# Reading the last 64 rows of the second wq as eight groups of sixteen half rows

## The chip, the cores and the metric

The kernel runs on one core of a Trainium2 chip. The metric is the device time of one execution in microseconds, here the median of three runs. One further execution was taken by the hardware profiler; durations and times of single steps come from it.

## What is computed

Two independent problems, A and B, of the same shapes are computed one after the other: one decoding step of attention over a sliding window. Per problem:

```python
# x [2, 1, 576], k_cache and v_cache [2, 16, 16384, 128], wq [576, 4096], wo [4096, 576], all bf16
W = 4096                                     # the last 4096 positions of the cache
q = (x @ wq).reshape(B, 1, 32, 128)          # 32 query heads, 16 key heads
scores = einsum(q, k[last W]) * 128 ** -0.5  # each key head serves two query heads
o = einsum(softmax(scores), v[last W])
result = o.reshape(B, 1, 4096) @ wo          # [2, 1, 576]
```

The output is both results side by side.

## The kernel before

Nearly all of the data is read once: per problem 32 MB of keys, 32 MB of values and twice 4.5 MB of weights. The caches are read as slabs of 4 MB, `K0` to `K15` and `V0` to `V15` (eight of each per problem); a slab holds one key head in each of four (batch, head group) places, with 32 KB for each of 128 partitions. Slabs go into the ring buffer `ring`, which has four places. Everything large is issued by SyncE (SP) on one queue, in the order of a list `stream`: both wq first, then K0, K1, V0, K2, V1 and so on, and at the end K14, K15, V13, V14, V15. A slab's issue (line 246) waits for the last reader of the slab four places before. The last slab, V15, comes in two pieces (line 242), of 96 and 32 of its 128 columns of keys, each with a semaphore of its own; behind it stand the last rows of wo (lines 282 and 267). The small outputs of problem A are issued on the same queue after that (line 708).

Per K slab, VectorE transposes the slab in four parts (`xt`, line 460), TensorE computes scores (`st`, lines 483 and 167), VectorE takes the maximum, ScalarE the exponential, and VectorE lays the result out for the product with the V slab (`acc`, line 575). That product runs one to two slabs behind. ScalarE evicts it (`acc_sb`, line 587), TensorE combines it (`ot`, line 604, for the last slab line 594), and after every second slab a projection with wo follows (line 690). The outputs are cast (lines 698 and 699) and written (line 708).

The queries come first. wq has 576 rows. Its first 512 are read as one slab of 4 MB into `ring` (line 255), four rows to a partition. The last 64 rows have 8 KB each; they are read in half rows of 4 KB, one to each of 128 partitions, into `wqr` (line 253): partition 2r + h holds half h of row r. A column of the first half of the output may use only the partitions of the first half rows. So the matching column of x is spread with zeros: `x_dup` holds two vectors of 128 values, one for each half h, with x at the partitions 2r + h and 0 at the others. `f_xd` (line 361) writes x into them, TensorE transposes them together with the four chunks of the rest of x (line 354), ScalarE copies the six results into `xT` (line 369), and line 413 multiplies chunk by chunk.

Of the kernel before, what the change touches and what calls it, by code (L numbers as in the profile page):

```python
# [6 lines left out]
BF16 = mybir.dt.bfloat16  # L7
# [52 lines left out]
def build_kernel(nc, probs, out, cfg=None):  # L60
# [8 lines left out]
    NPROB = len(probs)  # L69
    Bb, _one, D = x0.shape  # L70
# [15 lines left out]
    NFC = D // 128  # L86
    DREM = D - 128 * NFC
    assert DREM * 2 == 128 and NFC * HD == SLABW
    HH = HD // 2
    NXC = NFC + 2  # L90
    NOUT = wo0.shape[1]
    NH = NOUT // 2
    ACC0 = 128
# [12 lines left out]
    with es:  # L106
        block = es.enter_context(nc.Block())
        sb = lambda name, shape, dt: es.enter_context(nc.sbuf_tensor(name, shape, dt))
        ring = sb("ring", [128, NR, SLABW], BF16)
        xt = sb("xt", [128, NKT, 2048], FP32)  # L110
        wqr = sb("wqr", [128, NPROB, HH], BF16)
        wob = sb("wob", [128, 2, 8, NOUT], BF16)
        xT = sb("xT", [128, NXC, NPROB, 128], BF16)
        x_dup = sb("x_dup", [NPROB * Bb, 2, DREM, 2], BF16)
        x_sb = sb("x_sb", [NPROB * Bb, D], BF16)
        ident_b = sb("ident_b", [128, 128], BF16)
        zq = sb("zq", [128, 4, NZQ, ZW], BF16)
# [40 lines left out]
        wq_sem = [sem("wq%d" % r) for r in range(NPROB)]  # L158
# [6 lines left out]
        def matmul_again(e, first, out_ap, rhs, start, stop, skip=True):  # L165
            i = first.ins
            return e.add_instruction(mybir.InstMatmult(  # L167
                name=nc.get_next_instruction_name(), engine=i.engine, ins=[e.lower_ap(rhs), i.ins[1]], outs=[e.lower_ap(out_ap)],
                start_tensor_calc=start, stop_tensor_calc=stop, tile_size=i.tile_size, tile_position=i.tile_position,
                bass_skip_group_check=skip, ldweights=False))  # L170

        S = _Sched()
        dma_count = {}

        def dma_op(eng, sem_h, n_dmas, fn, deps, tag):
            op = S.add(eng, fn, deps, tag)
            dma_count[sem_h] = dma_count.get(sem_h, 0) + 16 * n_dmas
            op.dma = (sem_h, dma_count[sem_h])
            return op

        def load_x(P, eng):
            return dma_op(eng, x_sem[P], 1, lambda e: e.dma_start(
                x_sb[P * Bb:(P + 1) * Bb, :], probs[P][0][:, 0, :]).then_inc(x_sem[P], 16), [], "xload%d" % P)
# [14 lines left out]
        p_mrow = S.add("pool", lambda e: e.affine_select(  # L198
            mrow[:].rearrange("k (x c r) -> k x c r", c=4, r=2), ones_b[0:4, :].rearrange("k (x c r) -> k x c r", c=4, r=2),
            [[0, 16], [1, 4], [0, 2]], ALU.is_equal, 0.0, base=0, channel_multiplier=-1), [p_ones_b], "mrow")  # L200
        x_zd = S.add("dve", lambda e: e.memset(x_dup[:].rearrange("b h r t -> b (h r t)"), 0.0), [], "zero_xdup")

        stream = [("Q", P) for P in range(NPROB)]
        for s_ in range(ND + LS):
# [44 lines left out]
        def issue_wq(n, P):  # L249
            wqP = probs[P][3]  # L250
            r = n % NR
            deps = [reader[n - NR]] if n >= NR else []
            wq_dma[P] = dma_op("sp", wq_sem[P], 1, lambda e: e.dma_start(
                wqr[:, P, :], wqP[NFC * 128:D, :].rearrange("r (h n) -> r h n", h=2)).then_inc(wq_sem[P], 16), [], "wqr%d" % P)
            slab_dma[n] = dma_op("sp", ring_sem[r], 1, lambda e: e.dma_start(
                ring[:, r, :], wqP[0:NFC * 128, :].rearrange("(p s) n -> p (s n)", s=NFC)).then_inc(ring_sem[r], 16), deps, "wq%d" % P)

            if P == 0:
                for P_ in range(1, NPROB):
                    x_dma[P_] = load_x(P_, "sp")  # L260
# [27 lines left out]
        def issue_until(n_needed):  # L288
            while nxt[0] <= n_needed:
                for G in w_at.pop(stream[nxt[0]], []):  # L290
                    issue_wo(G)
                issue_slab(nxt[0])
                nxt[0] += 1
# [25 lines left out]
        def tb_job(fn, tag, deps):  # L319
            n = tbn[0]  # L320
            tbn[0] += 1
            bank = TB[n % NTB]
            d = list(deps)
            if n >= NTB:
                d.append(tb_consumer[n - NTB])
            return n, bank, S.add("pe", lambda e: fn(e, bank), d, tag)
# [18 lines left out]
        def f_xT(e, bank):  # L345
            last = None
            bb = bank[:].bitcast(BF16)
            NB = NPROB * Bb
            for ch in range(NXC):
                if ch < NFC:  # L350
                    src = x_sb[0:NB, 0:NFC * 128].rearrange("b (p s) -> b s p", s=NFC)[:, ch, :]
                else:
                    src = x_dup[0:NB, ch - NFC, :, :].rearrange("b r t -> b (r t)")
                last = e.transpose(bb[:, ch * NB:(ch + 1) * NB], src, ident_b[0:NB, 0:NB])  # L354
            return last
        issue_until(0)
        init_small()
        def f_xd(e):
            last = None
            for hf in range(2):  # L360
                last = e.tensor_copy(x_dup[:, hf, :, hf], x_sb[:, NFC * 128:D])  # L361
            return last
        x_cd = S.add("dve", f_xd, [x_zd] + list(x_dma.values()), "xdup")

        n_x, bank_x, op_xT = tb_job(f_xT, "xT", list(x_dma.values()) + [x_cd, p_ident_b])

        def f_xev(e):
            NB = NPROB * NXC
            return e.activation(
                xT[:].rearrange("c h p (a w) -> c (h p) a w", a=4)[:, :, :, 0:Bb],  # L370
                bank_x[:].bitcast(BF16)[:, 0:NB * Bb].rearrange("c (p b) -> c p b", b=Bb).unsqueeze(2).broadcast_to([128, NB, 4, Bb]),
                ACTF.Copy)
# [22 lines left out]
        def do_qproj(G):  # L395
            P = G // GPP
            nq = pos[("Q", P)]
            issue_until(nq)
            evs = []
            for nb in range(2):  # L400
                hf = nb
                c0 = nb * HH + 512 * (G % GPP)

                def fn(e, bank, c0=c0, hf=hf, nb=nb):
                    last = None
                    chs = list(range(NFC - 1)) + [NFC, NFC - 1]
                    for k_, ch in enumerate(chs if nb == 0 else chs[::-1]):
                        w_ = ring[:, nq % NR, ch * HD + c0:ch * HD + c0 + 512] if ch < NFC else wqr[:, P, c0 - hf * HH:c0 - hf * HH + 512]
                        x_ = xT[:, ch if ch < NFC else NFC + hf, P, :]
                        if k_ == 0 and q_first[0] == (P, ch):  # L410
                            last = matmul_again(e, q_first[1], bank[:, 0:512], w_, True, False, False)
                        else:
                            last = q_first[1] = e.matmul(bank[:, 0:512], x_, w_, start=(k_ == 0), stop=(k_ == NFC))  # L413
                        q_first[0] = (P, ch)
                    return last
                n, bank, op = tb_job(fn, "q%d_%d" % (G, nb), [slab_dma[nq], wq_dma[P], op_xev])
                qproj[(G, nb)] = op
                reader[nq] = op
                d = [op]
                if G >= 1:  # L420
                    d.append(chain[(G - 1, "qtr")])
                evs.append(S.add("act", lambda e, bank=bank, nb=nb: e.activation(qrow[:, 512 * nb:512 * nb + 512], bank[:, 0:512], ACTF.Copy),  # L422
                                 d, "qrow%d_%d" % (G, nb)))
                tb_consumer[n] = evs[-1]
            d = list(evs)
            if G >= 1:
                d.append(qkeep[G - 1])
            chain[(G, "qtr")] = S.add("dve", lambda e: e.transpose(qtr[:].bitcast(FP32), qrow[:].bitcast(FP32)), d, "qtr%d" % G)  # L428

            def f_keep(e):  # L430
                last = None
                v = qtr[:].rearrange("d (t l r f w p) -> d l w t r f p", t=2, l=2, r=2, f=2, w=32)
                o = qk[:, G, :, :, :].rearrange("d l (f p) (b t r) -> d l b t r f p", f=2, b=Bb, t=2)
                for l_ in range(2):
                    for b in range(Bb):
                        last = e.activation(o[:, l_, b], v[:, l_, b], ACTF.Copy)  # L436
                return last
            qkeep[G] = S.add("act", f_keep, [chain[(G, "qtr")]], "qkeep%d" % G)
# [358 lines left out]
        for e in ENGS:  # L797
            n = 0
# [77 lines left out]
def bass_concat_heads__sliding_block_cached__sliding_block_cached__decode_kernel(  # L876
    nc, A_x, A_k_cache, A_v_cache, A_wq, A_wo, B_x, B_k_cache, B_v_cache, B_wq, B_wo, out,
):
    build_kernel(nc, [(A_x, A_k_cache, A_v_cache, A_wq, A_wo), (B_x, B_k_cache, B_v_cache, B_wq, B_wo)], out)
# [28 lines left out]
```

## Time and profile before

| | |
|---|---|
| median of three runs | 366.08 us (365.82 to 366.17) |
| profiled execution, first to last instruction (span) | 364.5 us |
| median less span | 1.6 us |
| DMA | 153.27 MB, 420 GB/s over the span |
| PE busy | 219.7 us (60%) |
| DVE busy | 198.6 us (54%) |
| ACT busy | 67.8 us (19%) |
| POOL busy | 16.4 us (4%) |
| chain that ended last | DMA 70%, DVE 14%, PE 12%, ACT 2% |

PE is TensorE's matrix multiplication, PEld its loading of weights, DVE VectorE, ACT ScalarE, POOL GpSimd and SP SyncE. A row of the timeline has its start, its duration, the engine, the line, the operation, what it writes and reads, the shape, how many there are in one row, and in brackets how long the engine had been idle before and what ended that. The chain that ended last is followed back from the last instruction, at each step to what released it. The profile has no time of its own for the profiled execution beyond its span; the runs' median is set beside it.

### The profile page before, as it was taken

The numbers are of one execution on the slowest core, as the hardware profiler recorded it, in microseconds if no ns is written. First come the engines' busy times: TensorE is split into PE (matmuls) and PEld (weight loads), VectorE is DVE, ScalarE is ACT, GpSimd is POOL, SyncE is SP. The second block draws the span as 40 slices with busy tenths as digits, with TensorE's granted clock in tenths as the row PEclk, the third lists the DMA queues.
The fourth block names the chain that finished last, engine by engine and source line by source line (L and its number), as shares of the span: only waits on it lengthen the run. The fifth ranks groups of instructions, "written<-read, shape, count | busy, mean of one in ns | idle before, by whom it ended". The sixth has DMA issues, their size and how long they took to land.

```text
span 364.5 us, 2971 instructions
## 1 busy us (share of the span) xinstructions
PE 219.7 (60%) x1370; PEld 64.7 (18%) x1097; DVE 198.6 (54%) x173; ACT 67.8 (19%) x155; POOL 16.4 (4%) x45
## 2 busy tenths in 40 slices
PE   0399687291837657192955749083764828286866
PEld 0023112020211212021211212021221202021132
DVE  2022895574909375382917568291926557199620
ACT  1047203020300303020200303020210303011211
POOL 5000000000000000000000000000000000000000
PEclk9999899697885969687685969889696969869985
DMA  8999999999999999999999999999999999999993
GB/s 345 432 432 435 428 409 457 414 453 408 440 435 428 433 412 447 424 433 428 427 445 421 442 424 424 430 432 432 422 450 421 442 421 423 439 421 442 415 419 136
DMA packets 7075, 153.27 MB, mean 420 GB/s; under 512 B 780, under 2 KB 1304, under 8 KB 1688
## 3 DMA queue, kind: packets, MB, share of 16 engines
q1 hardware_dynamic: 7056, 153.10, 98.1%
q8 instruction: 9, 0.15, 0.2%
q10 hardware_dynamic: 8, 0.00, 0.0%
q14 instruction: 2, 0.02, 0.0%
HBM read 153.10 MB, written 0.00 MB: 420 GB/s over the span
## 4 chain that ended last, share of the span: by engine, by line
DMA 70%; DVE 14%; PE 12%; ACT 2%; issue 0%; SPq 0%; DVEq 0%
DMA ring<-in_B_k_cache_dram 34%; DMA ring<-in_A_k_cache_dram 25%; DVE xt L460 13%; DMA ring<-in_B_v_cache_dram 8%; PE st L483 4%; PE st L167 3%; DMA x_sb<-in_B_x_dram 3%; PE tb L413 3%; ACT qrow L422 1%; PE tb L167 1%; DVE qtr L428 1%; PE ot L690 1%; DVE nM L506 1%; ACT qk L436 0%; PE tb L496 0%
## 5 line engine op out<-in xcount | busy, mean ns | idle before, releaser
L460 DVE STREAM_TRANSPOSE xt<-ring 128x2048 f32<-128x2048 f32 x64 | 144.9, 2285 | 108.3 <-DMA ring<-in_B_k_cache_dram 59.4
L483 PE MATMUL st<-xt,zq 128*128 128x512 bf16 x256 | 113.0, 442 | 121.5 <-DVE xt L460 121.2
L167 PE MATMUL st<-xt,zq 128*128 128x512 bf16 x256 | 111.9, 437 | 0.0
L483 PEld LDWEIGHTS st<-xt,zq 128*128 128x128 bf16 x256 | 27.3, 107 | 209.7 <-DVE xt L460 138.5
L511 ACT ACTIVATE nMrep<-nM 1x128 f32<-1x128 f32 x16 | 4.9, 308 | 176.5 <-DVE nM L506 176.5
L575 PE MATMUL acc<-ring,pC 128*32 128x512 bf16 x512 | 34.1, 403 | 1.3 <-DMA ring<-in_B_v_cache_dram 1.3
L536 DVE STREAM_TRANSPOSE pC<-pR 128x1024 bf16<-128x1024 bf16 x16 | 19.4, 1214 | 3.7 <-ACT pR L528 2.1
L587 ACT ACTIVATE acc_sb<-acc 128x512 bf16<-128x512 f32 x16 | 9.5, 596 | 62.8 <-PE acc L575 62.8
L493 DVE TENSOR_REDUCE m<-st 128x1 f32<-128x1024 f32 x16 | 19.0, 1190 | 1.0 <-PE st L167 0.9
L528 ACT ACTIVATE pR<-st,bias_sb 128x1024 bf16<-128x1024 f32 x16 | 17.8, 1113 | 0.5
L413 PE MATMUL tb<-ring,xT 128*128 128x512 bf16 x50 | 16.5, 419 | 0.1
L575 PEld LDWEIGHTS acc<-ring,pC 128*32 128x32 bf16 x512 | 13.2, 100 | 17.3 <-issue 6.2
L428 DVE STREAM_TRANSPOSE qtr<-qrow 128x512 f32<-128x512 f32 x8 | 5.7, 711 | 19.1 <-ACT qrow L422 19.1
L544 POOL TENSOR_SCALAR rsel<-maskS,rsum 128x8 f32<-128x8 bf16 x16 | 4.9, 306 | 243.1 <-ACT pR L528 243.1
L391 ACT ACTIVATE st<-maskB 128x1024 f32<-128x1024 bf16 x14 | 14.4, 1028 | 0.4
L447 POOL TENSOR_TENSOR zq<-qk,maskA 128x128 bf16<-128x128 bf16 x16 | 6.3, 398 | 86.8 <-PE st L167 69.5
L690 PE MATMUL ot<-wob,Rsb 128*2 128x288 bf16 x120 | 9.8, 309 | 0.3 <-ACT Rsb L670 0.3
L422 ACT ACTIVATE qrow<-tb 128x512 bf16<-128x512 f32 x16 | 9.2, 586 | 3.6 <-PE tb L413 3.3
L354 PE MATMUL tb<-ident_b,x_sb 4*128 4x4 bf16 x4 | 0.3, 173 | 14.8 <-DVE x_dup L361 14.8
L413 PEld LDWEIGHTS tb<-ring,xT 128*128 128x128 bf16 x50 | 5.1, 105 | 11.5 <-issue 7.5
L413 PE MATMUL tb<-wqr,xT 128*128 128x512 bf16 x16 | 6.6, 411 | 0.0
L361 DVE COPY x_dup<-x_sb 4x64 bf16<-4x64 bf16 x2 | 0.3, 190 | 11.5 <-DMA x_sb<-in_B_x_dram 11.5
(64 smaller groups left out, 83.3 us busy)
## 6 DMA issues: line engine op xcount, KB each, us to landing
ring<-in_A_k_cache_dram SPq DMA_DIRECT2D x8, 4096.0 KB, 30.5
ring<-in_A_v_cache_dram SPq DMA_DIRECT2D x8, 4096.0 KB, 35.3
ring<-in_B_k_cache_dram SPq DMA_DIRECT2D x8, 4096.0 KB, 30.7
ring<-in_B_v_cache_dram SPq DMA_DIRECT2D x7, 4096.0 KB, 35.2
wob<-in_A_wo_dram SPq DMA_DIRECT2D x4, 1152.0 KB, 37.1
ring<-in_A_wq_dram SPq DMA_DIRECT2D x1, 4096.0 KB, 12.8
ring<-in_B_wq_dram SPq DMA_DIRECT2D x1, 4096.0 KB, 21.8
wob<-in_B_wo_dram SPq DMA_DIRECT2D x3, 1152.0 KB, 37.4
```

Of the source, the lines that this page charges most:

```text
L167: return e.add_instruction(mybir.InstMatmult(name=nc.get_next_instruction_name(), engine=i.engine, ins=[e.lower_ap(rhs), i.ins[1]], outs=[ ...
L391: chain[(s, "fill")] = S.add("act", lambda e: e.activation(ST[s % 2][:, :].rearrange("k (h j) -> k h j", h=2), maskB[:].unsqueeze(1).broad ...
L413: last = q_first[1] = e.matmul(bank[:, 0:512], x_, w_, start=(k_ == 0), stop=(k_ == NFC))
L422: evs.append(S.add("act", lambda e, bank=bank, nb=nb: e.activation(qrow[:, 512 * nb:512 * nb + 512], bank[:, 0:512], ACTF.Copy), d, "qrow% ...
L460: Xop[(s, u)] = S.add("dve", lambda e: e.transpose(xt[:, i % NKT, :].rearrange("k (j w) -> k j w", w=64), ring[:, n % NR, :].bitcast(FP32) ...
L483: first = last = e.matmul(bank, zq[:, p4, s % NZQ, w0:w0 + 128], mv, start=False, stop=stop, skip_group_check=True)
L493: chain[(s, "max")] = S.add("dve", lambda e: e.tensor_reduce(m1[:, 0:1], ST[s % 2][:, :], AX.X, ALU.max), d, "max%d" % s)
L528: chain[(s, "exp")] = S.add("act", lambda e: e.activation(pR[:, :], ST[s % 2][:, :], ACTF.Exp, bias=bias_sb[:, 0:1], scale=SCALE, accum_ou ...
L536: chain[(s, "pC")] = S.add("dve", lambda e: e.transpose(pC[:, s % NPT, :, :].rearrange("k j c -> k (j c)"), pR[:, :]), d, "pC%d" % s)
L575: last = e.matmul(ACC[32 * cb:32 * cb + 32, 0:512], pC[:, D_ % NPT, j0_:j0_ + 4, :].rearrange("k j c -> k (j c)"), ring[:, n % NR, j0_ * 1 ...
L587: acc_ev[D_] = S.add("act", lambda e: e.activation(acc_sb[:], ACC[:, :], ACTF.Copy), d, "accev%d" % D_)
L690: last = e.matmul(proj_out(half), l_, wob[:, pc, s_, half * NH:(half + 1) * NH], start=False, stop=True, skip_group_check=True)
```

## The change

For problem B (P == 1) the 64 rows are read in another order. Row r = 4i + r' (r' from 0 to 3) and half h go to partition 16(2r' + h) + i instead of 2r + h: the DMA's source has an outermost dimension of eight, the pairs (r', h), and in each of them sixteen half rows. The bytes read are the same. Problem A keeps its order.

`x_dup` gets two more vectors, in which x of problem B is spread in the new order; both problems' x are written into all four vectors, and each problem uses its own two. TensorE transposes eight vectors instead of six, and `xT` grows from six to eight chunks.

```diff
-    NXC = NFC + 2
+    NXC = NFC + 4
...
-        x_dup = sb("x_dup", [NPROB * Bb, 2, DREM, 2], BF16)
+        x_dup = sb("x_dup", [NPROB * Bb, 4, 128], BF16)
...
+            rest = wqP[NFC * 128:D, :]
+            rest = rest.rearrange("r (h n) -> r h n", h=2) if P == 0 else rest.rearrange("(i r) (h n) -> (r h) i n", r=4, h=2)
             wq_dma[P] = dma_op("sp", wq_sem[P], 1, lambda e: e.dma_start(
-                wqr[:, P, :], wqP[NFC * 128:D, :].rearrange("r (h n) -> r h n", h=2)).then_inc(wq_sem[P], 16), [], "wqr%d" % P)
+                wqr[:, P, :], rest).then_inc(wq_sem[P], 16), [], "wqr%d" % P)
...
-                    src = x_dup[0:NB, ch - NFC, :, :].rearrange("b r t -> b (r t)")
+                    src = x_dup[0:NB, ch - NFC, :]
...
             for hf in range(2):
-                last = e.tensor_copy(x_dup[:, hf, :, hf], x_sb[:, NFC * 128:D])
+                xr = x_sb[:, NFC * 128:D]
+                e.tensor_copy(x_dup[:, hf, :].rearrange("b (r t) -> b r t", t=2)[:, :, hf], xr)
+                last = e.tensor_copy(x_dup[:, 2 + hf, :].rearrange("b (r t i) -> b r t i", r=4, t=2)[:, :, hf, :],
+                                     xr.rearrange("b (i r) -> b r i", r=4))
...
-                        x_ = xT[:, ch if ch < NFC else NFC + hf, P, :]
+                        x_ = xT[:, ch if ch < NFC else NFC + 2 * P + hf, P, :]
```

More of the change, by code (lines that the diff above doesn't have):

```diff
@@ L200, in build_kernel @@
             [[0, 16], [1, 4], [0, 2]], ALU.is_equal, 0.0, base=0, channel_multiplier=-1), [p_ones_b], "mrow")
-        x_zd = S.add("dve", lambda e: e.memset(x_dup[:].rearrange("b h r t -> b (h r t)"), 0.0), [], "zero_xdup")
+        x_zd = S.add("dve", lambda e: e.memset(x_dup[:].rearrange("b v p -> b (v p)"), 0.0), [], "zero_xdup")
         stream = [("Q", P) for P in range(NPROB)]
```

## The prediction

> **What bounds the kernel now.** I read the page first (busy shares, DMA slices, queues), then the chain that ended last, then the timeline of its last 50 us and of the first 40, and at last the trace's DMA records: each packet, and for each DMA the times at which its sixteen engines reported their share as landed.
>
> ```profile
> DMA  8999999999999999999999999999999999999993
> ...
> q1 hardware_dynamic: 7056, 153.10, 98.1%
> q8 instruction: 9, 0.15, 0.2%
> ```
>
> The sixteen DMA engines are busy from the second slice to the last but one; PE has 60% and DVE 54%. The kernel is a DMA stream with a short tail. The second queue line matters more than its 0.2%: nine packets of instructions.
>
> ```profile
> 329.43 28.85 DMA ring<-in_B_v_cache_dram
> 358.28 0.04 issue
> 358.32 1.07 PE acc L575 x7
> 359.39 0.02 issue
> 359.42 0.61 ACT acc_sb L587
> ...
> 362.39 0.45 DVE out_sb L698
> ```
>
> The chain's last stretch: the second piece of the last V slab lands at 358.28, and from there to the end stands a fixed tail (PV, eviction, combination, projection, cast, output). What lands before 358.28 by x brings the end forward by x, unless PE isn't ready for it. How ready PE is stands in the timeline:
>
> ```profile
> 317.92 2.31 DVE L460 STREAM_TRANSPOSE xt<-ring 128x2048 f32<-128x2048 f32 x1 [9.49 <-DMA ring<-in_B_k_cache_dram]
> ...
> 354.45 0.26 PE L604 MATMUL ot<-ident_r,acc_sb 128*128 128x8 bf16 x4 [0.71 <-ACT acc_sb L587]
> ...
> 355.79 2.20 PE L575 MATMUL acc<-ring,pC 128*32 128x512 bf16 x24 [1.08 <-DMA ring<-in_B_v_cache_dram]
> ...
> 357.92 0.21 PE L662 MATMUL tb<-mask4S,om 128*128 128x4 bf16 x2
> ...
> 358.32 1.04 PE L575 MATMUL acc<-ring,pC 128*32 128x512 bf16 x8 [0.19 <-DMA ring<-in_B_v_cache_dram]
> ```
>
> PE waits 1.08 us for the first piece and only 0.19 us for the second. The first line is the start of what makes PE ready: DVE idles 9.49 us for slab K14, and from there to 354.71 I find the work back to back (transposes, scores, maximum, exp, the last but one PV): no wait in it ends with a DMA.
>
> Now the completions, by engine (my sorting of the trace's records; us):
>
> ```
> DMA (landing)              eight early engines   the other eight
> first wq slab              13.54 .. 14.10 (all sixteen)
> second wqr (the change's)  14.83 .. 15.41 (all sixteen)
> K14                        316.07 .. 317.07      317.66 .. 317.90
> V15, first piece           352.51 .. 353.51      354.11 .. 354.34, one 355.74
> V15, second piece          355.01 .. 356.00      356.59 .. 356.85, one 358.28
> last wo rows               357.92 .. 358.91      359.46 .. 359.70, one 361.08
> ```
>
> The engines start together, within 0.56 us, and end 3.3 us apart. The nine instruction packets do it: 16 KB each, 1.02 to 1.10 us, at 46, 84, 127, 161, 190, 230, 270, 310 and 349 us. After each, one engine's landings are 1.4 us behind (54.25 was the last but one and 55.42 the last after the first packet; two were at 97.07 and 97.14 after the second). Eight packets fell on eight different engines, the ninth on one of these again. That engine alone sets 358.28.
>
> **The change part by part.** *The DMA.* wqr of the second problem takes, engine by engine, 14.83 - 13.54 = 1.29 us for 32 KB. On eight engines it is 64 KB each: these come 1.29 us later from 15 us on, the others 1.29 us earlier; total bytes stay. Which eight? The change's own words give the number only. The two-row outputs of the first problem wait in the same queue behind the last wo rows; their packets on their two engines begin at 357.92 and 358.13, when only early engines are through. I take it that the eight begin with the same two and are the early ones. [...]
>
> The end is then set so:
> - K14: the later of 317.07 + 1.29 = 318.36 and 317.90 - 1.29 = 316.61. It lands 0.46 us later than now, since it came before the ninth packet. PE is ready for the last V slab at 354.71 + 0.46 = 355.17.
> - V15, first piece: the later of 353.51 + 1.29 = 354.80 and 355.74 - 1.29 = 354.45. So PE starts at 355.17 to 355.20 instead of 355.79, and no longer waits for the DMA.
> - Its 24 matmuls and the redistribution took 355.79 to 358.13, 2.34 us: done at 357.52.
> - Second piece: the later of 356.00 + 1.29 = 357.29 and 358.28 - 1.29 = 356.99; there before 357.52. Its PV starts at 357.52 instead of 358.32: 0.80 us won.
> - Last wo rows: the later of 358.91 + 1.29 = 360.20 and 359.79. Their two matmuls are the last of eight from 361.18 (1.17 us), near 362.0 now and 361.2 then: covered.
>
> Bounds: were the path from K14 slack, the landing would decide, 358.28 - 357.29 = 0.99 us. Were the 64 KB slower, each tenth of 2.58 us adds 0.26 us to K14 and takes as much from the gain; the first wqr shows this size of packet with the queue just starting and cannot settle it.
>
> *The x side.* Two more DVE copies (0.30 us for the two there now), two more PE transposes (0.19 for two), a third more for ACT's copy of xT (0.25 now, so +0.05 to 0.1), for Pool's clearing of xT (0.73, so +0.24) and twice the clearing of x_dup (0.17, below +0.17):
>
> ```profile
> 14.41 0.30 DVE L361 COPY x_dup<-x_sb 4x64 bf16<-4x64 bf16 x2 [11.51 <-DMA x_sb<-in_B_x_dram]
> 14.93 0.19 PE L354 MATMUL tb<-ident_b,x_dup 4*128 4x4 bf16 x2
> 15.15 0.25 ACT L369 ACTIVATE xT<-tb 128x96 bf16<-128x96 bf16 x1 [11.74 <-PE tb L354]
> 28.60 0.54 SPq L246 DMA_DIRECT2D ring<-in_A_v_cache_dram  x1
> 38.20 0.54 SPq L246 DMA_DIRECT2D ring<-in_A_k_cache_dram  x1
> ```
>
> The two clearings lie in the 11 us before x lands. Copies, transposes and xT delay the projections by 0.5 to 0.6 us, and with them the two slab issues at 28.60 and 38.20 that wait for the projections. The V slab issued at 28.60 begins to move when K1 has landed at 44.5, K2 issued at 38.20 after V0 at 55.4: 16 and 17 us of cover. If that cover were gone, the whole 0.6 us would be paid. The second problem's projections start at 28.6; its wq lands at 25.1, then 26.4: covered by 2 us. PE's instruction count changes by a handful, so the packets keep their times. Sum of these: nothing.
>
> The span is 364.5 us, the median of three runs 366.08, 1.6 us around it that the change doesn't touch: 363.7 and 365.3.
>
> **The rivals.** *Engines that meet where they write (slower).* Each engine writes sixteen neighbouring partitions now, one 4 KB row after the other, while the other eight stream their wq rows into all they serve. If two engines write at one entry of the memory they take turns: 4 x 1.29 = 5.16 us for the 64 KB, 3.87 us later than now; three in turn 7.74, 6.45 later. K14 would land at 320.9 or 323.5, PE be ready 3.0 or 5.6 us later, and after the 2.34 us the end is 1.8 to 4.4 us late: 367.9 to 370.4, near 368.6 if engines get out of step and share part of the time. It decides as soon as the 64 KB take over 2.58 + 0.80 us. For it: each engine moves 32 KB packets at 1.218 us, 26.9 GB/s, without any sign of room beside its own share. Against it: no row shows two engines slowing each other. [...]
>
> *The wrong eight (slower).* If the eight engines are those with instruction packets, the last landing goes to 358.28 + 1.29, and the end to 367.4. The two early outputs speak against it.
>
> *It isn't eight.* If the transfer still runs on sixteen engines, only the hidden x work stays: 366.1.
>
> **How the numbers follow.** Balanced engines, my forecast: 0.60, with a time of 365.3 and a range of its own from 365.0 (the landing decides) to 365.7 (the 64 KB a seventh slower, clock of PE, which was granted 0.79 there). A run of this kernel tells 0.2%, 0.73 us, from no change, and the forecast of 0.80 lies just beyond it: 0.40 of the 0.60 go to faster, 0.18 to no change, 0.02 to slower. Engines that meet: 0.27, of which 0.25 slower and 0.02 no change. The wrong eight: 0.09, slower. Not eight: 0.04, no change. So faster 0.40, no change 0.24, slower 0.36. The range goes from 364.9 to 369.2, which leaves out the worst third of the meeting engines and little else.
>
> **What would show it.** Right: eight of the second wqr's engines land it near 16.2, the others report nothing for it; K14 lands near 318.4; the wait of 1.08 us before the last V slab's PV is gone, its second piece starts near 357.5 with all landings between 356 and 357.3. Wrong: the wqr needs 4 us or more after 14.1 and the K slabs from then on land 3 us late on some engines (they meet); the last landing near 359.6 (wrong eight); a first piece still waited for; first slab issues moved with DMA slices below 9 near 55 us.

## The result: slower by 1.1%

The changed kernel takes 370.2 us (five runs, 369.1 to 370.7) against 366.1 us before: a ratio of 1.011 (95% interval 1.0098 to 1.0122). The profiled execution after has a span of 367.0 us against 364.5, 2.5 us more; the runs' median moved by 4.1. The two profiled executions aren't alike: the one after is the fastest of its five runs (369.1 us), and the one before had its last matrix products at a granted clock of 0.50 (359 to 363 us), where the one after had 1.00. Over all runs the median span is 367.2 us after and 363.7 before (from the runs of the kernel before that were taken with the experiments), 3.5 us apart; why the times differ by more than that isn't shown.

From the page of the changed kernel, the rate over the 40 slices, and the two queues:

```profile
GB/s 343 282 404 454 404 452 415 443 414 448 406 437 432 446 413 421 446 438 418 416 456 420 436 436 436 405 450 421 421 433 452 418 439 417 449 407 454 414 418 192
...
q1 hardware_dynamic: 7048, 153.10, 98.4%
q8 instruction: 9, 0.15, 0.2%
```

Bytes and instruction packets are the same. The second slice (9 to 18 us) has 282 GB/s (432 before), where every later one but the last has over 400. The stretch from 14 to 20 us, before and after (time, length, busy time of PE, PEld, DVE, ACT and POOL with instructions, PE's clock, DMA share, GB/s):

```profile
14.00:20.00 6.00, 5.23 (x18) 1.33 (x15) 0.30 (x2) 1.45 (x3) 0.00 (x0) 1.00 1.11 478
```

```profile
14.00:20.00 6.00, 5.19 (x20) 1.38 (x17) 0.49 (x4) 1.47 (x3) 0.00 (x0) 1.00 0.95 195
```

DMA is as busy as ever (0.95) and moves 195 GB/s instead of 478. (A packet's bytes count where it starts: spread over each packet's duration, the bytes before give 432 GB/s in this stretch, not 478, and those after 194.) In the trace's DMA records the 4 KB packets of the second wqr take 320 to 490 ns in this stretch, against 159 at their start; the other eight engines' 32 KB packets of the wq slab that begin between 13.2 and 16.5 us take 2.5 to 3.0 us, against 1.21. The busy share doesn't tell the packets that moved from those that were held up.

The end of the chain, and the steps of the timeline that the prediction was made from:

```profile
336.21 28.28 DMA wob<-in_B_wo_dram
364.49 0.04 issue
364.54 0.31 PE ot L695 x2
...
364.87 0.45 DVE out_sb L703
```

```profile
322.73 2.31 DVE L465 STREAM_TRANSPOSE xt<-ring 128x2048 f32<-128x2048 f32 x1 [9.51 <-DMA ring<-in_B_k_cache_dram]
...
359.05 0.26 PE L609 MATMUL ot<-ident_r,acc_sb 128*128 128x8 bf16 x4 [0.71 <-ACT acc_sb L592]
359.23 1.48 PE L580 MATMUL acc<-ring,pC 128*32 128x512 bf16 x24
...
361.70 0.62 PE L580 MATMUL acc<-ring,pC 128*32 128x512 bf16 x8 [0.85 <-DMA ring<-in_B_v_cache_dram]
...
364.54 0.08 PEld L695 LDWEIGHTS ot<-wob,oTn 128*2 128x2 bf16 x2 [0.28 <-DMA wob<-in_B_wo_dram]
```

K14 is taken up at 322.73 instead of 317.92, 4.8 us later. PE is ready for the last V slab at 359.31 instead of 354.71, 4.6 us later, and starts without a wait. The second piece is waited for (0.85 us), and the last wo rows, at 364.49 instead of 361.08, set the end. The eight matmuls on the second piece took 0.62 us here, at a granted clock of 1.00, and 1.04 before, at 0.50: the tail that the prediction called fixed differed with the clock.

### The profile page after: what moved, and what is told of

Read it like the earlier page. It is cut to its first block, busy times and chain, and to the rows that moved or that the text cites. A ratio compares the mean times of both kernels' runs of the same rounds, so it can differ in the third digit from the quotient of the medians.

```text
span 367.0 us, 2977 instructions
## 1 busy us (share of the span) xinstructions
PE 217.4 (59%) x1372; PEld 64.2 (17%) x1099; DVE 198.9 (54%) x175; ACT 67.7 (18%) x155; POOL 16.6 (5%) x45
## 4 chain that ended last, share of the span: by engine, by line
DMA 74%; DVE 14%; PE 9%; SPq 1%; ACT 0%; issue 0%
DMA ring<-in_B_k_cache_dram 34%; DMA ring<-in_A_k_cache_dram 26%; DVE xt L465 13%; DMA wob<-in_B_wo_dram 8%; DMA ring<-in_B_wq_dram 7%; PE st L488 4%; PE st L167 3%; PE tb L418 2%; DVE nM L511 1%; PE tb L167 0%; PE tb L501 0%; SPq L242 0%; SPq L255 0%; SPq L269 0%; ACT qrow L427 0%
## 5 line engine op out<-in xcount | busy, mean ns | idle before, releaser
L488 PEld LDWEIGHTS st<-xt,zq 128*128 128x128 bf16 x256 | 27.2, 106 | 212.1 <-DVE xt L465 142.6
L580 PEld LDWEIGHTS acc<-ring,pC 128*32 128x32 bf16 x512 | 13.2, 99 | 16.9 <-issue 6.4
## 6 DMA issues: line engine op xcount, KB each, us to landing
ring<-in_A_wq_dram SPq DMA_DIRECT2D x1, 4096.0 KB, 13.2
```

The source lines that it names most:

```text
L488: first = last = e.matmul(bank, zq[:, p4, s % NZQ, w0:w0 + 128], mv, start=False, stop=stop, skip_group_check=True)
L580: last = e.matmul(ACC[32 * cb:32 * cb + 32, 0:512], pC[:, D_ % NPT, j0_:j0_ + 4, :].rearrange("k j c -> k (j c)"), ring[:, n % NR, j0_ * 1 ...
```

## The experiments

The theory: engines **meet** where they write, as the first rival had it. Against it stood the order in which the source is read, the number of engines, and the x side. In the tables and texts "the eight" are the engines that carry the second wqr: eight land it in the changed kernel (19.99 to 20.24), sixteen before (14.83 to 15.41). Which engine writes which partitions isn't in the trace; where it is said below, it is my reading of each DMA's order, and so is who meets whom.

**The x side alone (e1).** Edits against the changed kernel:

```diff
-            rest = rest.rearrange("r (h n) -> r h n", h=2) if P == 0 else rest.rearrange("(i r) (h n) -> (r h) i n", r=4, h=2)
+            rest = rest.rearrange("r (h n) -> r h n", h=2)
...
-                        x_ = xT[:, ch if ch < NFC else NFC + 2 * P + hf, P, :]
+                        x_ = xT[:, ch if ch < NFC else NFC + hf, P, :]
```

> Only the x side of the change: four spread vectors, eight transposes, eight chunks of xT; the second wqr is read in the old order on sixteen engines. Both theories: the x side is hidden, 366.1 us as before (365.8 to 366.4), the second wqr lands at 15.4 on all sixteen. If the x side cost something, the first matmuls would show it and the time would be above 366.4.

Measured: 365.82 us, ratio 0.9993 (0.9983 to 1.0003). The first of the four copies and the first projection in its timeline:

```profile
14.05 0.19 DVE L364 COPY x_dup<-x_sb 4x64 bf16<-4x64 bf16 x1 [11.01 <-DMA x_sb<-in_B_x_dram]
...
16.65 1.46 PE L418 MATMUL tb<-ring,xT 128*128 128x512 bf16 x3
```

From the first copy to the first projection it is 2.60 us, where it was 2.36 (14.41 to 16.77): 0.24 us more, and not the 0.5 to 0.6 of the prediction. The projection still starts earlier, since x itself was there 0.36 us earlier in this execution. The time of the kernel shows no cost.

**Meeting or source order (e2, e3, e4).** e2 keeps the source's spacing and the eight engines, but goes by 32 partitions at a time, so that each DMA gives an engine four neighbours:

```diff
+                    for j in range(4):
+                        last = e.dma_start(wqr[32 * j:32 * j + 32, P, :], rest[16 * j:16 * j + 16, :].rearrange(
+                            "(i r) (h n) -> (r h) i n", r=4, h=2)).then_inc(wq_sem[P], 16)
```

> Eight engines and 64 KB each as in the change, source rows with the same spacing of 32 KB, but as four DMAs of 32 partitions, so that an engine writes four neighbouring partitions in each and the eight engines never share a group of 32 in the pattern of the change. Engines that meet where they write: in the first two DMAs nobody meets (1.29 us), in the last two each of the eight meets one of the other eight (2.58 us): wqr lands 3.9 us after the first wq, near 18.0, instead of 20.1, the other eight lose 1.3 us, the time is near 367.3. Source order (eight engines that read 4 KB pieces 32 KB apart in step slow all reading): nothing changes, wqr near 20, time 369.5 to 370.5.

e3 keeps the destination and reads 64 KB in one stretch per engine:

```diff
+            rest = wqP.rearrange("(g q) (h n) -> g q h n", g=8, h=2)[:, 0:8].rearrange("g q h n -> g (q h) n")
```

> Destination as in the change (eight groups of sixteen partitions, one engine each), but each engine reads 64 KB in one stretch: the first eight rows of each 72 of wq, so the remainder of problem B is multiplied with other rows. Engines that meet where they write: as the change, wqr near 20, time 369.5 to 370.5. Source order: wqr takes 2.6 to 3 us, lands near 16.8, the other eight are where they were or earlier, the time is 365.5 to 366.5.

e4 is the change with r=16 in the place of r=4 (DMA and x):

> Source order on sixteen engines: 32 groups of four half rows, 128 KB apart within a group, x spread to fit; each engine has 32 KB as before and writes the same partitions as before. Engines that meet where they write: nobody meets, wqr lands at 15.4, 366.1 us. Source order: the sixteen need 2.5 us or more instead of 1.29, all slabs move by over 1.2 us and the time is 367.3 or more.

Measured: e2 367.11 us, 1.0040 (1.0025 to 1.0055); e3 370.36, 1.0126 (1.0095 to 1.0157); e4 365.80, 1.0002 (0.9992 to 1.0012). All three as meeting has it: reading in one stretch doesn't help, and reading with gaps doesn't hurt. e2 shows it DMA by DMA. The eight engines' completions of its four DMAs, from the trace (us; the first wq ends at 13.47 to 13.87):

```
partitions 0-31     14.12 .. 14.28    0.65 us after the first wq
partitions 32-63    14.84 .. 15.12    about 0.7
partitions 64-95    16.17 .. 16.43    1.3
partitions 96-127   17.33 .. 17.56    1.1
```

16 KB per engine took 0.65 us in the lower half of memory and 1.1 to 1.3 in the upper, where by my reading the other eight are writing their slab. The other eight are held up as well: their next slab lands at 24.5 to 24.8, where 1.29 us less than before would be 23.3 to 23.8.

**The amount without meeting (e5), and two ways of meeting (e6, e7).** Whole rows of 8 KB, 64 partitions, multiplied as one chunk of 64 rows; only partitions differ, and in e6 that one DMA stands for two (the rows lie in a part of `xt` that isn't in use yet):

```diff
 # e5: lower half, two DMAs of 32 partitions      (e7: the same at partitions 64 to 127)
+                    for j in range(2):
+                        last = e.dma_start(wql[32 * j:32 * (j + 1), :],
+                                           rest[32 * j:32 * (j + 1), :].rearrange("(i r) n -> r i n", r=8)).then_inc(wq_sem[P], 16)
 # e6: lower half, one DMA of 64 partitions
+                    last = e.dma_start(wql[0:64, :], rest.rearrange("(i r) n -> r i n", r=8)).then_inc(wq_sem[P], 16)
```

> The amount that the change moves (64 KB on each of eight engines, nothing on the others), but whole rows into partitions 0 to 63 in two DMAs of 32 partitions, four neighbouring partitions for each engine, the lower half of memory only. Engines that meet where they write: nobody meets, the eight land the second wqr near 16.1, the other eight are 1.3 us earlier than before from there on. For the time the two halves of my prediction part: if the eight carry no instruction packets, 365.2; if two of them do, as the completions after the change let me think, these two end 1.3 us later than before, K14 lands 1.1 us later, and the time is 365.9 to 366.3. If eight engines alone made it slow, wqr lands near 20 and the time is near 370.

> As e5, but one DMA of 64 partitions, eight neighbouring partitions for each engine: if the memory is entered every 32 partitions at the same place, engines 0 and 4, 1 and 5, 2 and 6, 3 and 7 meet and the other eight are left alone. Engines that meet where they write: the eight land near 18.6 (16.1 if they keep out of step), the other eight as in e5; the time is 367.5 to 368.8. Without such meeting: as e5.

> As e5, but partitions 64 to 127, which the other eight engines write with every slab. Engines that meet where they write: each of the eight meets one of the others: 64 KB in 5.0 us, landing near 18.6, and the other eight lose 2.5 us; the time is 367.8 to 368.8. Without such meeting: as e5.

Measured: e5 365.54 us, 0.9983 (0.9974 to 0.9993): faster than both kernels. e6 367.63, 1.0042 (1.0026 to 1.0057); e7 367.78, 1.0045 (1.0029 to 1.0062). The same stretch from 14 to 20 us in e5, e6 and e7:

```profile
14.00:20.00 6.00, 5.64 (x21) 1.52 (x18) 0.30 (x4) 1.47 (x3) 0.00 (x0) 1.00 1.04 448
```

```profile
14.00:20.00 6.00, 4.96 (x19) 1.22 (x16) 0.41 (x3) 1.42 (x3) 0.00 (x0) 1.00 0.93 277
```

```profile
14.00:20.00 6.00, 5.47 (x22) 1.42 (x18) 0.47 (x4) 1.47 (x3) 0.00 (x0) 1.00 0.93 273
```

The bytes, rows and engines are the same in all three; 448, 277 and 273 GB/s is what the partitions make of them. e7 is as expected (18.64 to 18.76, the other eight 25.9 to 26.3). One part of e6's expectation failed. The eight do land near 18.6 (18.05 to 18.67), but the other eight, whom by my reading no one meets there, are late as well: 25.6 to 26.0 for the next slab, where e5 has 23.3 to 23.6.

**Meeting on sixteen engines (e8).** The change with r=8: groups of eight half rows.

> Sixteen engines, 16 groups of eight half rows for eight neighbouring partitions each, 32 KB on each engine as before. Engines that meet where they write: two engines share each place, wqr takes up to 2.6 us instead of 1.3 on all sixteen, everything after it is up to 1.3 us later, the time is 366.8 to 367.4. Number of engines or source order as the cause: as before, 366.0.

Measured: 366.90 us, 1.0023 (1.0012 to 1.0034); the second wqr lands at 15.85 to 16.38 on all sixteen, 1.0 us later than before. So it isn't the number of engines.

**Another's place, without meeting (e10), and a meeting of two (e11).** e10 moves both DMAs of e5 to partitions 16 to 47; e11 has a single DMA on two engines:

```diff
 # e10
+                        last = e.dma_start(xtb[16:48, HD * (j + 1):HD * (j + 2)],
+                                           rest[32 * j:32 * j + 32, :].rearrange("(i r) n -> r i n", r=8)).then_inc(wq_sem[P], 16)
 # e11
+                    last = e.dma_start(xtb[0:4, :], rest[0:12, :].rearrange("(i r s) n -> r i (s n)", r=2, s=3)).then_inc(wq_sem[P], 16)
```

> As e5 in bytes and engines, but both DMAs of 32 partitions go to partitions 16 to 47, so that each of the eight engines writes where another one usually writes, and no two of them the same place. The last 64 rows are left out of problem B's queries. Meeting as the cause: nobody meets while the eight run together, they land near 16.1, the others at their 23.3 for the next slab, the time is 365.3 to 365.8. If what costs is writing at a place that is not the engine's own: as e6, the eight near 18.6, the others near 25.7, 367.3 to 367.9.

> Only two engines get a share of the second wqr's DMA, 48 KB each, both into partitions 0 to 3, where the first of them writes its slabs; the rest of the 64 rows isn't read and is left out of problem B's queries. It asks whom a meeting of two delays. If only those who meet: the two take 3.6 us and land near 17.2, the other fourteen land the next slab at 23.3. If the memory's path is held up for all, as e6 looks: the other fourteen lose about as much as the two lose by meeting, 1.8 us, and land at 25.1.

Measured: e10 lands at 16.01 to 16.16, as e5 (15.96 to 16.09), and the other eight at 23.40 to 23.66; its time is 365.87 us, 1.0002 (0.9986 to 1.0019), a little above what was expected and no different from the kernel before. Writing at another engine's place cost nothing here, with that engine elsewhere. In e11 the two land at 17.26 and 17.27, the 17.2 expected for twice the time of 48 KB (1.8 us, an estimate from the 1.215 us that a 32 KB packet took before), and the other fourteen at 23.19 to 23.66: nobody else is held up (365.51 us, 0.9987, 0.9977 to 0.9998, with fewer bytes read).

**Half the amount (e9).** 32 rows as in e5, on partitions 0 to 31; the other 32 as quarter rows over all 128 partitions:

```diff
+                    e.dma_start(wql[0:32, :], rest[0:32, :].rearrange("(i r) n -> r i n", r=8)).then_inc(wq_sem[P], 16)
+                    return e.dma_start(wqr[:, HH:HH + HD // 4], rest[32:64, :].rearrange("r (h n) -> r h n", h=4)).then_inc(wq_sem[P], 16)
```

> Half the shift of e5, nobody meets: 32 of the 64 rows as whole rows into partitions 0 to 31 on eight engines (32 KB each), the other 32 as quarter rows over all 128 partitions on sixteen (16 KB each); the eight get 0.65 us more than before, the others 0.65 us less. Engines that meet where they write, with two of the eight carrying instruction packets: the second wqr lands near 15.5 on the eight and 14.9 on the others after the part that all share; the last landing falls from 361.2 to 360.6, since the engine with two packets gives 0.65 and the two of the eight get it; K14 lands 0.5 us later; the time is 365.3 to 365.7, as e5 within 0.2. If no engine of the eight carried packets, it would end behind e5 (365.6 to 365.8).

Measured: 365.57 us, 0.9989 (0.9975 to 1.0003); the last landing is at 360.54, K14 at 318.25. As expected, but no better than e5 and not clear of no change.

The landings together (us, last of each group; "both" where the groups don't part):

| | second wqr | next slab, other eight | next slab, the eight | K14 | last wo rows | time |
|---|---|---|---|---|---|---|
| before | 15.41 | 25.11 both | | 317.90 | 361.08 | 366.1 |
| changed | 20.24 | 27.54 | 29.81 | 322.71 | 364.49 | 370.2 |
| e2, four DMAs | 17.56 | 24.81 | 27.14 | 319.95 | 362.33 | 367.1 |
| e3, source in one stretch | 20.36 | 27.88 | 29.89 | 322.88 | 366.19 | 370.4 |
| e5, nobody meets | 16.09 | 23.57 | 25.80 | 319.11 | 360.89 | 365.5 |
| e6, pairs among the eight | 18.67 | 25.95 | 28.40 | 321.10 | 362.89 | 367.6 |
| e7, one of each eight | 18.76 | 26.30 | 28.39 | 321.44 | 363.19 | 367.8 |
| e8, sixteen engines | 16.38 | 26.10 both | | 318.94 | 362.09 | 366.9 |

## Why the prediction was wrong

**The step that failed: "On eight engines it is 64 KB each: these come 1.29 us later from 15 us on, the others 1.29 us earlier."** The bytes per engine were right, the time for them wasn't: I doubled 1.29 us as if an engine's own rate were the only limit. After the first wq's last landing (14.10 before, 14.49 after) the eight need to 20.24, about 6 us from their own starts near 14, not 2.58. The other eight land the next slab at 27.2 to 27.5, where 1.29 us less would have been 23.3 to 23.8: they lose some 3.8 us by work that isn't theirs. All else follows from this: K14 4.8 us late, PE ready 4.6 us late, the end carried by the last rows on the engines that were delayed most.

**The first rival was what happened.** It had 367.9 to 370.4 and 0.27; 370.2 came, in part by chance: the rival had the end come from PE's readiness, and here the last wo rows set it. That the cause lies where the engines write is shown by e5, e7 and e10, with the same bytes on the same engines and only the partitions different (last landing of the second wqr at 16.09, 18.76 and 16.16; 365.5, 367.8 and 365.9 us), and by e2, which has the change's half rows with its spacing at full rate in the lower half (0.65 us a DMA, against 1.1 to 1.3 in the upper). That a meeting of two halves their rate agrees with e7 and e11, by my reading of who meets whom. e3 and e4 rule out the order of the source. I gave the rival less than half the chance of the plain sum because no row showed two engines slowing each other. The rows couldn't: the large DMAs before the change ran at their full rate (4224 packets of 32 KB, 1.215 us in the median, all but 20 of them under 1.3).

**The rival's own sizes were off.** It had 5.16 us for the 64 KB if two take turns and 7.74 if three do; the other eight should have lost 1.29 by the same reckoning, an estimate from the bytes (the upper 64 partitions get 256 KB, 32 KB for each of them). No run shows three engines in turn, from which the 7.74 us and the 370.4 came: all of the eight needed about 6, and the others lost 3.8. e6 shows the same: by my reading no one meets the other eight there, and they lose 2.4 us, nearly the 2.6 of those that meet, while in e11 a meeting of two delays nobody else. Why the others lose it, and from how many meetings on, stays open; no run tells it. Nor does any run have an engine write eight or sixteen neighbours without meeting another: in the changed kernel, e3, e6 and e8 the two come together, and a cost of the many neighbours themselves isn't ruled out there. e7 and e11 show meeting alone, with four neighbours or fewer to an engine.

**"I take it that the eight ... are the early ones" was right for six of eight.** e5 shows it, where nothing else is disturbed. The completions of V14, the slab after K15 and V13, in its trace:

```
other eight    344.09 344.43 | 345.67 345.70 345.74 345.75 345.81 345.86
the eight      346.54 346.57 346.68 346.77  347.28 347.56 | 348.11 348.26
```

Eight instruction packets had passed by then. Six fell on the other eight, and two on engines of the eight (348.11 and 348.26, 1.5 us behind 346.6); what put 347.28 and 347.56 behind isn't shown. The two early outputs that I argued from stand for two engines only. Moving 1.29 us to the eight therefore makes the last of them the new end: 360.89, nearly the 361.08 of before. In e5 the end is the last wo rows:

```profile
333.04 27.85 DMA wob<-in_B_wo_dram
360.89 0.04 issue
360.93 0.31 PE ot L710 x2
```

So even the amount that I forecast, placed where nobody meets, gave 0.56 us (365.54 against 366.10) and not 0.80.

**What held.** The x side is hidden (e1). No wait for a DMA lies between K14 and the last V slab: K14 moved by 4.81 us and PE's readiness by 4.60. But the length of that stretch isn't fixed, as "354.71 + 0.46" took it to be: from the first transpose of K14 to PE's readiness it is 36.8 us before, 35.9 in e1 and 35.7 in e5, where K14 comes 1.2 us later and PE is ready only 0.1 us later. The 28 matmuls of the last but one PV alone took 3.01 us before and 2.31 in e5. A gain of 0.80 us read from one execution is smaller than this spread. The range, to 369.2, cut off the upper part of the very rival that came true.

## What to carry to other kernels

The number of engines and the bytes of each didn't give the DMA's time here: 64 KB on each of eight engines landed at 16.09 in e5 and at 20.24 in the changed kernel. Ask for every engine which partitions it writes and who else writes there at that time: four neighbours per engine, by 32 partitions at a time, ran at full rate here in the lower half of memory (e5, 448 GB/s from 14 to 20 us) and not in the upper (e7, 273); with sixteen neighbours all engines together moved 195. When a stream's end is set by a few late engines, find out which they are from more than two samples before moving bytes onto the others; and when a rival with a mechanism has no row against it, let the range reach to its end.

## What the runs showed of the hardware that was not expected

By my reading of who writes where, a meeting of DMA engines cost engines that took no part in it 2.4 us each in e6. In the changed kernel the other eight lost 3.8, and all together moved 165 to 183 GB/s from 14 to 18 us, where it was 431 before (from the trace's packets, each spread over its duration). A meeting of only two engines (e11) cost no one else anything: the other fourteen landed the next slab at 23.19 to 23.66, against 23.40 to 23.66 for the other eight in e10. Instruction packets of 16 KB, of 1.02 to 1.10 us, each held one engine up by 1.4 us. In the kernel before there are nine: the first eight fall on eight different engines and the ninth on one of these again; in e5 six of the first eight are in one half of the engines and two in the other.
